# Softmax row sums moved from a ones-matmul on TensorE to GpSimd's sum across partitions

## The chip, the cores and the metric

The kernel runs on one core of one Trainium2 chip. The metric is device time in microseconds (us), where lower is better. Unless a single run is named, a time is the median of several runs. A ratio is the mean time of one kernel's fast runs over that of the other kernel's fast runs of the same rounds, so it is not quite the ratio of the medians that stand beside it. The experiments ran in three sets of rounds, on three chips; the kernel before ran in each set and took 368.65 to 368.81 us (medians), so times of different sets can be compared to a few tenths of a us.

PE is TensorE's matmul stream and PEld its weight loads, DVE is VectorE, ACT is ScalarE, POOL is GpSimd and SP is SyncE.

## The reference

Two independent problems A and B of the same shape are computed and their outputs concatenated. Each is grouped-query attention against a cache, with a projection before and after:

```python
# B=16, Sq=32, D=1024, Hq=32, Hkv=4, Sk=512, Dh=128, all bf16
q = (x @ wq).reshape(B, Sq, Hq, Dh).transpose(0, 2, 1, 3)
k, v = jnp.repeat(k_cache, 8, axis=1), jnp.repeat(v_cache, 8, axis=1)
scores = jnp.einsum("bhqd,bhkd->bhqk", q, k) * Dh ** -0.5
p = softmax(scores, axis=-1)
o = jnp.einsum("bhqk,bhkd->bhqd", p, v)
out = o.transpose(0, 2, 1, 3).reshape(B, Sq, Hq * Dh) @ wo
```

## The kernel before

The attention part is 128 slots. A slot handles one group: one batch row and one key head, with 8 query heads x 32 positions = 256 query columns and 512 keys in 4 chunks of 128. Scores lie transposed, keys on partitions, so the softmax sum runs over chunks (VectorE) and over partitions (a matmul with a constant matrix of ones). Each slot also issues 7 "filler" matmuls of the projections. These are Q-projection matmuls in the first 64 slots (66 in the changed kernel) and output-projection matmuls after them. I call the two stretches the Q stage and the output stage and part them at slot 70.

```python
def partial_sums(i):                      # VectorE: add the 4 key chunks
    p_sb = st[i]["p"]                     # [128, 4 chunks, 256 columns] bf16
    t1 = work.tile([P, 2, QW], FP32, name="t1")
    nc.vector.tensor_tensor(out=t1[:], in0=p_sb[:, 0:2, :], in1=p_sb[:, 2:4, :], op=ALU.add)
    t = work.tile([P, QW], FP32R, name="t")
    nc.vector.tensor_tensor(out=t[:], in0=t1[:, 0, :], in1=t1[:, 1, :], op=ALU.add)
    st[i]["t"] = t

def values(i):
    ...
    for c in range(KC):                   # 4 values matmuls
        nc.tensor.matmul(ob[:, 0:QW], lhsT=v_sb[:, i % GRP, c, :], rhs=d["p"][:, c, :],
                         start=(c == 0), stop=(c == KC - 1))
    nc.tensor.matmul(ob[:, QW:2 * QW], lhsT=ones[:], rhs=d["t"][:], start=True, stop=True)
    ...
    nc.scalar.activation(out=lg[:, q, :], in_=ob[:, QW:2 * QW], func=ACTF.Ln)
    nc.scalar.activation(out=r[:], in_=lg[:, q, :], func=ACTF.Exp, scale=-1.0)
    ...

for i in range(2 * NG):                   # 128 slots
    do_loads(i)
    scores(i)                             # 4 matmuls, then Exp on ScalarE into p_sb
    run(units, 4)                         # 4 filler matmuls
    if i > 0:
        values(i - 1)
    partial_sums(i)
    run(units, 3)                         # 3 filler matmuls
    if i > 0:
        normalize(i - 1)                  # VectorE: oT <- r * ob
```

After the loop a test decides at run time whether a slower general path has to repeat everything. With these inputs it never does.

Of the kernel before, what the change touches and what calls it, by code (L numbers as in the profile page):

```python
# [1 line left out]

# [5 lines left out]

BF16 = mybir.dt.bfloat16
FP32 = mybir.dt.float32  # L10
# [6 lines left out]
P = 128  # L17
# [5 lines left out]
SCALE = float(DH) ** -0.5  # L23

SHIFT = 44.0
ONES = 2.0 ** -75
LIMIT = 20.0


# [143 lines left out]
def kernel(  # L173
# [25 lines left out]
    NG = B * HKV  # L199
    BPT = P // SQ  # L200
    QW = REP * SQ

    out_flat = out.flatten_outer_dims()
    problems = [
# [4 lines left out]
    def fast_path(ok_i):  # L209
        with ExitStack() as fctx:  # L210
            enter = fctx.enter_context
            const = enter(tc.tile_pool(name="const", bufs=1))
            blk = enter(tc.tile_pool(name="blk", bufs=20))
            kv = enter(tc.tile_pool(name="kv", bufs=2))
            work = enter(tc.tile_pool(name="work", bufs=2))
            outp = enter(tc.tile_pool(name="outp", bufs=3))
# [6 lines left out]
            warm = const.tile([P, NW], BF16, name="warm")  # L223
            nc.vector.memset(warm[:], 0.0)  # L224
            ident = const.tile([P, P], BF16, name="ident")
            make_identity(nc, ident[:])
            ones_f = const.tile([P, P], FP32, name="ones_f")
            nc.vector.memset(ones_f[:], ONES)
            ones = const.tile([P, P], FP32R, name="ones")
            nc.vector.tensor_copy(out=ones[:], in_=ones_f[:])  # L230
            one_col = const.tile([P, 1], FP32, name="one_col")
            nc.vector.memset(one_col[:], 1.0)
            shift = const.tile([P, 1], FP32, name="shift")
            nc.vector.memset(shift[:], SHIFT)
            cnt = const.tile([P, 1], FP32, name="cnt")
            nc.vector.memset(cnt[:], 0.0)
            NLR = 2 * NG // GRP
            lall = const.tile([NLR, GRP * QW], FP32, name="lall")


            def blk_tile(shape, name, dtype=BF16):
# [23 lines left out]
            def load_kv(j):  # L265
                pr, jj = divmod(j, NG // GRP)
                k, v = problems[pr][1], problems[pr][2]
                kT = kv.tile([P, GRP, SK], BF16, name="kT")
                v_sb = kv.tile([P, GRP, KC, DH], BF16, name="v_sb")
                if pr == 0:  # L270
                    g, b0 = divmod(jj * GRP, B)
                    ks, vs = k[b0:b0 + GRP, g], v[b0:b0 + GRP, g]
                    for q in range(GRP):
                        nc.sync.dma_start_transpose(out=kT[:, q, :], in_=ks[q])
                else:
                    ks, vs = k[jj], v[jj]
                    nc.sync.dma_start_transpose(
                        out=kT[:], in_=ks.rearrange("g k d -> (g k) d")
                    )
                nc.sync.dma_start(  # L280
                    out=v_sb[:], in_=vs.rearrange("q (p c) d -> p q c d", c=KC)
                )
                kv_tiles[j] = (kT, v_sb)
# [27 lines left out]
            def f_units(pr, tt, nh, last=False):  # L311
                ps = psum.tile([P, NW], FP32, name="f_ps", tag="proj")
                for h in range(HQ):
                    nc.tensor.matmul(  # L314
                        ps[:],
                        lhsT=oT[pr, tt][:, h, :],
                        rhs=wo_tiles[pr, nh, h // REP][:, h % REP, :],
                        start=(h == 0),
                        stop=(h == HQ - 1),
                    )  # L320
                    if h == HQ - 1:
                        o_sb = outp.tile([P, NW], BF16, name="o_sb")
                        nc.vector.tensor_copy(out=o_sb[:], in_=ps[:])  # L323
                        c0 = problems[pr][5] + nh * NW
                        (nc.sync if last else nc.gpsimd).dma_start(  # L325
                            out=out_flat[tt * P:(tt + 1) * P, c0:c0 + NW], in_=o_sb[:]
                        )
                    yield

            def run(units, n):  # L330
# [14 lines left out]
            def scores(i):  # L345
                pr, b, g = where(i)
                kT = kv_tiles[i // GRP][0].rearrange("p q (k c) -> p q c k", c=KC)
                s_ps = psum.tile([P, KC, QW], FP32, name="s_ps", tag="s")
                for c in range(KC):
                    nc.tensor.matmul(  # L350
                        s_ps[:, c, :],
                        lhsT=kT[:, i % GRP, c, :],
                        rhs=qT[pr, g][:, b, :, :].rearrange("p h s -> p (h s)"),
                        start=True,
                        stop=True,
                    )
                p_sb = work.tile([P, KC, QW], BF16, name="p_sb", bufs=3)
                nc.scalar.activation(  # L358
                    out=p_sb[:], in_=s_ps[:], func=ACTF.Exp, bias=shift[:], scale=SCALE
                )  # L360
                st[i] = {"p": p_sb}

            def partial_sums(i):
                p_sb = st[i]["p"]
                t1 = work.tile([P, 2, QW], FP32, name="t1")
                nc.vector.tensor_tensor(
                    out=t1[:], in0=p_sb[:, 0:2, :], in1=p_sb[:, 2:4, :], op=ALU.add
                )
                t = work.tile([P, QW], FP32R, name="t")
                nc.vector.tensor_tensor(  # L370
                    out=t[:], in0=t1[:, 0, :], in1=t1[:, 1, :], op=ALU.add
                )
                st[i]["t"] = t

            ltile = {}

            def values(i):
                d = st[i]
                v_sb = kv_tiles[i // GRP][1]
                ob = psum.tile([P, 2 * QW], FP32, name="ob", tag="ob")  # L380
                for c in range(KC):
                    nc.tensor.matmul(  # L382
                        ob[:, 0:QW],
                        lhsT=v_sb[:, i % GRP, c, :],
                        rhs=d["p"][:, c, :],
                        start=(c == 0),
                        stop=(c == KC - 1),
                    )
                nc.tensor.matmul(  # L389
                    ob[:, QW:2 * QW], lhsT=ones[:], rhs=d["t"][:], start=True, stop=True  # L390
                )
                d["ob"] = ob
                j, q = divmod(i, GRP)
                if q == 0:
                    ltile[j] = work.tile([P, GRP, QW], FP32, name="lg")
                lg = ltile[j]
                nc.scalar.activation(  # L397
                    out=lg[:, q, :], in_=ob[:, QW:2 * QW], func=ACTF.Ln
                )
                r = work.tile([P, QW], FP32, name="r")  # L400
                nc.scalar.activation(out=r[:], in_=lg[:, q, :], func=ACTF.Exp, scale=-1.0)  # L401
                d["r"] = r
                if q == GRP - 1:
                    nc.gpsimd.dma_start(  # L404
                        out=lall[j:j + 1, :],
                        in_=lg[0:1, :, :].rearrange("p q n -> p (q n)"),
                    )

            def normalize(i):
                pr, b, g = where(i)  # L410
# [2 lines left out]
                if (pr, tt) not in oT:  # L413
                    oT[pr, tt] = blk_tile([P, HQ, P], "oT")
                nc.vector.scalar_tensor_tensor(  # L415
                    out=oT[pr, tt][:, g * REP:(g + 1) * REP, bl * SQ:(bl + 1) * SQ],
                    in0=d["r"][:].rearrange("p (h s) -> p h s", s=SQ),
                    scalar=ONES,
                    in1=d["ob"][:, 0:QW].rearrange("p (h s) -> p h s", s=SQ),
                    op0=ALU.mult,  # L420
                    op1=ALU.mult,
                )
# [91 lines left out]
            def at(slot, fn, *args):  # L514
                plan.setdefault(slot, []).append((fn, args))

            for j in range(2, 2 * NG // GRP):
                at(GRP * (j - 1) + 1, load_kv, j)
            for c4 in range(3, 16):
                need = (c4 - 2) * 4 * DC / 7.0  # L520
                at(max(0, int(need) - 10), load_wq, c4 // 8, c4 % 8)
# [3 lines left out]
                nc.sync.dma_start_transpose(out=xT[1][:], in_=B_x.flatten_outer_dims())  # L525

            at(12, load_xT_b)
            for nh in range(NH):
                for hg in range(HKV):
                    at(NG - 12 + nh * 8 + hg * 2, load_wo, 0, nh, hg)  # L530
                    at(NG + 20 + nh * 18 + hg, load_wo, 1, nh, hg)

            def do_loads(i):
                for fn, args in plan.get(i, []):
                    fn(*args)


            for i in range(2 * NG):
                do_loads(i)
                scores(i)  # L540
                run(units, 4)
                if i > 0:
                    values(i - 1)
                partial_sums(i)
                run(units, 3)
                if i > 0:
                    normalize(i - 1)
            run(units, 4)
            values(2 * NG - 1)
            run(units, 4)  # L550
            normalize(2 * NG - 1)


            run(units, 8)
            sq = blk_tile([NLR, GRP * QW], "sq", FP32)
            nc.vector.tensor_tensor(out=sq[:], in0=lall[:], in1=lall[:], op=ALU.mult)
            nc.vector.tensor_scalar(
                out=sq[:], in0=sq[:], scalar1=LIMIT * LIMIT, scalar2=0.0,
# [11 lines left out]
    total = 2 * NG * QW  # L570
    ok = nc.values_load(ok_i[0:1, 0:1], min_val=0, max_val=total,
                        skip_runtime_bounds_check_because="only compared")
    with tc.If(ok < total, preferred_fallthrough_block=False):
        general_path(tc, problems, out_flat)


# [28 lines left out]
```

## Time and profile before

| | before |
|---|---|
| time | 368.72 us, median of 3 runs (368.47 to 369.12) |
| span of the profiled run, granted clock | 366.2 us, 0.995 |
| PE / DVE / ACT / POOL busy | 97 / 67 / 68 / 7% |
| slot length, from scores to scores | 2.52 us, all but the first |
| first scores to last scores; after that to the end | 319.5 us; 24.7 us |

From the page of the kernel before, the busy times (us, share of the span, number of instructions) and the chain of waits that ended last (share of the span by engine, then by engine, tile and line):

```profile
span 366.2 us, 6094 instructions
PE 356.6 (97%) x2236; PEld 225.0 (61%) x2236; DVE 244.2 (67%) x478; ACT 249.2 (68%) x389; POOL 25.1 (7%) x53
...
PE 97%; DVE 0%; ACT 0%; issue 0%
```

The chain is the argument that counts: followed back from the last instruction, it hardly ever leaves PE. A share of busy time alone would not prove that.

The timeline of one slot in the output stage of the kernel before (columns: start in us, duration in us, engine, line, operation, out<-in, shapes, count, and in brackets the idle time before it and what ended it):

```profile
201.66 0.60 PE L382 MATMUL ob<-p_sb,v_sb 128*128 128x256 bf16 x4
...
202.02 0.36 PE L389 MATMUL ob<-t,ones 128*128 128x256 f32 x1
202.15 0.69 DVE L366 TENSOR_TENSOR t_2599<-p_sb 128x512 f32<-128x512 bf16 x1 [0.96 <-ACT p_sb L358]
...
202.22 0.82 PE L314 MATMUL f_ps<-wo_sb,oT 128*128 128x512 bf16 x3
...
202.94 0.43 DVE L370 TENSOR_TENSOR t<-t_2599 128x256 fp32r<-128x256 f32 x1
...
203.29 0.42 DVE L415 SCALAR_TENSOR_TENSOR oT<-r,ob 128x256 bf16<-128x256 f32 x1
...
204.18 0.60 PE L382 MATMUL ob<-p_sb,v_sb 128*128 128x256 bf16 x4
```

The slot repeats after 204.18 - 201.66 = 2.52 us. PE has no bracket: it never idles. The ones-matmul L389 is recorded as 0.36 us, but the next matmul starts 0.20 us after it, so the record overlaps its neighbours. What it costs PE must be read from starts.

### The profile page before, as it was taken

Reading aid. Unit: us, or ns where it says so; the run is one execution under the profiler, and the core shown is the slowest. Engines: PE = TensorE matmul, PEld = TensorE weight load, DVE = VectorE, ACT = ScalarE, POOL = GpSimd, SP = SyncE. Lnnn points to the kernel's source line nnn. Section 1 sums busy time; section 2 is a strip of 40 time slices with the busy share of each in tenths; the row PEclk is TensorE's granted clock in tenths of the full one; section 3 lists DMA queues with packets and bytes.
Section 4 is the critical chain, followed back from the end, with each engine's and each line's share of the span. In section 5 each row is a group of like instructions: output and inputs, shape, how many; then the busy total and the mean of one; then the engine's idle time right before and its main releaser. Section 6 shows DMA issues by size and latency. Waiting matters only on the chain.

```text
span 366.2 us, 6094 instructions
## 1 busy us (share of the span) xinstructions
PE 356.6 (97%) x2236; PEld 225.0 (61%) x2236; DVE 244.2 (67%) x478; ACT 249.2 (68%) x389; POOL 25.1 (7%) x53
## 2 busy tenths in 40 slices
PE   8999999999999999999999999999999999999990
PEld 5556666666666666666666666666666666666540
DVE  2458788887878787888856666666666676666530
ACT  3037777777777777777777777777777777777500
POOL 0000000000000000000001110110001111011100
PEclk9999999999999999999999999999999999999998
DMA  8998796977777784999995555799548974440000
GB/s 274 301 280 242 225 264 147 243 225 219 184 194 183 220 201 115 314 304 310 314 305 138 130 131 142 207 352 198 139 113 287 315 194 117 131 129 17 15 16 21
DMA packets 125974, 71.91 MB, mean 196 GB/s; under 512 B 74641, under 2 KB 124945, under 8 KB 125937
## 3 DMA queue, kind: packets, MB, share of 16 engines
q1 hardware_dynamic: 122848, 68.30, 67.5%
q0 software_dynamic: 1744, 2.10, 2.4%
q10 hardware_dynamic: 1344, 1.05, 0.9%
q8 instruction: 19, 0.31, 0.4%
q14 instruction: 19, 0.15, 0.1%
HBM read 51.38 MB, written 2.10 MB: 146 GB/s over the span
## 4 chain that ended last, share of the span: by engine, by line
PE 97%; DVE 0%; ACT 0%; issue 0%
PE f_ps L314 31%; PE q_ps L297 30%; PE s_ps L350 15%; PE ob L382 15%; PE ob L389 4%; PE warm_ps L446 1%; PE q_ps L469 1%; PE xT_ps L455 0%; ACT xT L460 0%; DVE o_sb L323 0%; DVE xT L459 0%; DVE warm L224 0%; PE ok_ps L563 0%
## 5 line engine op out<-in xcount | busy, mean ns | idle before, releaser
L358 ACT ACTIVATE p_sb<-s_ps,shift 128x1024 bf16<-128x1024 f32 x128 | 142.7, 1115 | 47.5 <-PE s_ps L350 47.5
L314 PE MATMUL f_ps<-wo_sb,oT 128*128 128x512 bf16 x512 | 132.8, 380 | 0.0
L297 PE MATMUL q_ps<-xT,wq_sb 128*128 128x512 bf16 x496 | 128.4, 380 | 0.0
L382 PE MATMUL ob<-p_sb,v_sb 128*128 128x256 bf16 x512 | 76.8, 273 | 0.0
L350 PE MATMUL s_ps<-qT,kT 128*128 128x256 bf16 x512 | 76.8, 273 | 0.0
L397 ACT ACTIVATE lg<-ob 128x256 f32<-128x256 f32 x128 | 49.5, 387 | 39.8 <-PE ob L389 39.8
L350 PEld LDWEIGHTS <-kT 128*128 128x128 bf16 x512 | 57.0, 113 | 28.3 <-issue 0.2
L382 PEld LDWEIGHTS <-v_sb 128*128 128x128 bf16 x512 | 50.1, 98 | 33.1
L314 PEld LDWEIGHTS <-oT 128*128 128x128 bf16 x512 | 44.6, 98 | 32.9
L297 PEld LDWEIGHTS <-wq_sb 128*128 128x128 bf16 x496 | 43.4, 97 | 31.9
L401 ACT ACTIVATE r<-lg 128x256 f32<-128x256 f32 x128 | 53.6, 418 | 4.0
L305 DVE CAST qT<-q_ps 128x512 bf16<-128x512 f32 x62 | 42.7, 689 | 18.2 <-PE q_ps L297 18.0
L415 DVE SCALAR_TENSOR_TENSOR oT<-r,ob 128x256 bf16<-128x256 f32 x128 | 53.5, 418 | 1.6 <-ACT r L401 1.6
L389 PE MATMUL ob<-t,ones 128*128 128x256 f32 x128 | 46.5, 363 | 0.0
L404 POOL DMA_DIRECT2D lall<-lg x32 | 15.9, 496 | 245.4 <-ACT lg L397 245.4
L389 PEld LDWEIGHTS ob<-t,ones 128*128 128x128 f32 x128 | 24.3, 190 | 1.4
L323 DVE CAST o_sb<-f_ps 128x512 bf16<-128x512 f32 x16 | 11.0, 689 | 9.0 <-PE f_ps L314 9.0
L325 POOL DMA_DIRECT2D out_dram<-o_sb x15 | 8.6, 571 | 81.3 <-DVE o_sb L323 81.3
L460 ACT COPY xT<-xT_ps 128x512 bf16<-128x512 bf16 x4 | 2.1, 590 | 5.1 <-DVE xT L459 5.1
L459 DVE COPY xT<-xT_ps 128x512 bf16<-128x512 bf16 x4 | 1.7, 426 | 5.3 <-PE xT_ps L455 5.3
L446 PE MATMUL warm_ps<-warm 128*128 128x512 bf16 x10 | 4.0, 560 | 1.2 <-DVE warm L224 1.2
L469 PE MATMUL q_ps<-xT,wq_sb 128*128 128x256 bf16 x32 | 4.0, 272 | 0.1
(280 smaller groups left out, 158.5 us busy)
## 6 DMA issues: line engine op xcount, KB each, us to landing
v_sb<-in_A_v_cache_dram SPq DMA_DIRECT2D x16, 512.0 KB, 4.2
wq_sb<-in_B_wq_dram SPq DMA_DIRECT2D x8, 1024.0 KB, 6.3
wo_sb<-in_A_wo_dram SPq DMA_DIRECT2D x8, 1024.0 KB, 7.5
v_sb<-in_B_v_cache_dram SPq DMA_DIRECT2D x16, 512.0 KB, 4.2
wo_sb<-in_B_wo_dram SPq DMA_DIRECT2D x8, 1024.0 KB, 8.9
wq_sb<-in_A_wq_dram SPq DMA_DIRECT2D x7, 1024.0 KB, 7.1
out_dram<-o_sb POOLq DMA_DIRECT2D x15, 128.0 KB, 2.4
kT<-in_A_k_cache_dram SPq DMA_TRANSPOSE x64, 3.1
```

The source lines that it names most:

```text
L297: nc.tensor.matmul(ps[:], lhsT=w[:, dc, (h % 4) * DH:(h % 4 + 1) * DH], rhs=xT[pr][:, dc, :], start=(dc == 0), stop=(dc == DC - 1),)
L305: nc.vector.tensor_copy(out=qT[pr, g][:, :, hl, :], in_=ps[:].rearrange("p (b s) -> p b s", s=SQ),)
L314: nc.tensor.matmul(ps[:], lhsT=oT[pr, tt][:, h, :], rhs=wo_tiles[pr, nh, h // REP][:, h % REP, :], start=(h == 0), stop=(h == HQ - 1),)
L323: nc.vector.tensor_copy(out=o_sb[:], in_=ps[:])
L350: nc.tensor.matmul(s_ps[:, c, :], lhsT=kT[:, i % GRP, c, :], rhs=qT[pr, g][:, b, :, :].rearrange("p h s -> p (h s)"), start=True, stop=True,)
L358: nc.scalar.activation(out=p_sb[:], in_=s_ps[:], func=ACTF.Exp, bias=shift[:], scale=SCALE)
L382: nc.tensor.matmul(ob[:, 0:QW], lhsT=v_sb[:, i % GRP, c, :], rhs=d["p"][:, c, :], start=(c == 0), stop=(c == KC - 1),)
L389: nc.tensor.matmul(ob[:, QW:2 * QW], lhsT=ones[:], rhs=d["t"][:], start=True, stop=True)
L397: nc.scalar.activation(out=lg[:, q, :], in_=ob[:, QW:2 * QW], func=ACTF.Ln)
L401: nc.scalar.activation(out=r[:], in_=lg[:, q, :], func=ACTF.Exp, scale=-1.0)
L404: nc.gpsimd.dma_start(out=lall[j:j + 1, :], in_=lg[0:1, :, :].rearrange("p q n -> p (q n)"),)
L415: nc.vector.scalar_tensor_tensor(out=oT[pr, tt][:, g * REP:(g + 1) * REP, bl * SQ:(bl + 1) * SQ], in0=d["r"][:].rearrange("p (h s) -> p h ...
```

## The change

The intent is to take the 128 ones-matmuls off TensorE, which bounds the kernel. GpSimd, only 7% busy until now, sums across partitions for two groups at a time. VectorE's two adds, which read two SBUF inputs each, become one reduce with a single input. Because the sums now come later, the values of a group are computed four slots behind its scores. Smaller parts: the identity matrix is made on VectorE, weight loads are rescheduled, the last output tile is copied and stored in halves, and the general path is laid out as the fall-through block of its branch.

```diff
+    LAG = 4
...
-                p_sb = work.tile([P, KC, QW], BF16, name="p_sb", bufs=3)
+                p_sb = work.tile([P, KC, QW], BF16, name="p_sb", bufs=LAG + 2)
...
             def partial_sums(i):
-                t1 = ...; tensor_tensor(out=t1, in0=p_sb[:, 0:2, :], in1=p_sb[:, 2:4, :])
-                t = ...;  tensor_tensor(out=t, in0=t1[:, 0, :], in1=t1[:, 1, :])
+                j, q = divmod(i, 2)
+                if q == 0:
+                    tsum[j] = work.tile([P, 2, QW], FP32, name="t")
+                nc.vector.tensor_reduce(
+                    out=tsum[j][:, q, :],
+                    in_=p_sb[:].rearrange("p c n -> p n c"),
+                    axis=AX.X, op=ALU.add,
+                )
+                if q == 1:
+                    sums[j] = work.tile([P, 2, QW], FP32, name="sums", bufs=3)
+                    nc.gpsimd.partition_all_reduce(sums[j], tsum.pop(j), channels=P,
+                                                   reduce_op=bass_isa.ReduceOp.add)
+            def reciprocals(j):                      # Ln, then Exp, on 512 columns
...
             def values(i):
-                nc.tensor.matmul(ob[:, QW:2 * QW], lhsT=ones[:], rhs=d["t"][:], ...)
...
+            for i in range(total_slots + LAG):
+                live = i < total_slots
+                if live:
+                    do_loads(i); scores(i)
+                if i % 2 == 1 and i >= 3:
+                    if i >= 5:
+                        keep_logs(i // 2 - 2)
+                    if i // 2 - 1 < NG:
+                        reciprocals(i // 2 - 1)
+                run(units, 4 if live else 5)
+                if i >= LAG:
+                    values(i - LAG)
+                if live:
+                    partial_sums(i)
+                run(units, 3 - (i % 4 == 3) if live else 3)
+                if i >= LAG:
+                    normalize(i - LAG)
...
-    with tc.If(ok < total, preferred_fallthrough_block=False):
+    with tc.If(ok < total, preferred_fallthrough_block=True):
```

More of the change, by code (lines that the diff above doesn't have):

```diff
@@ L4 @@
 import concourse.tile as tile
-from concourse import bass_utils, mybir
+from concourse import bass_isa, bass_utils, mybir
 from concourse._compat import with_exitstack
@@ L25 @@
 SHIFT = 44.0
-ONES = 2.0 ** -75
+DOWN = 2.0 ** -75
 LIMIT = 20.0
@@ L212, in fast_path @@
             const = enter(tc.tile_pool(name="const", bufs=1))
-            blk = enter(tc.tile_pool(name="blk", bufs=20))
+            blk = enter(tc.tile_pool(name="blk", bufs=19))
             kv = enter(tc.tile_pool(name="kv", bufs=2))
@@ L225, in fast_path @@
             ident = const.tile([P, P], BF16, name="ident")
-            make_identity(nc, ident[:])
-            ones_f = const.tile([P, P], FP32, name="ones_f")
-            nc.vector.memset(ones_f[:], ONES)
-            ones = const.tile([P, P], FP32R, name="ones")
-            nc.vector.tensor_copy(out=ones[:], in_=ones_f[:])
+            col = const.tile([P, P], BF16, name="col")
+            row = const.tile([P, P], BF16, name="row")
+            nc.vector.memset(row[:], 1.0)
+            nc.vector.tensor_tensor_scan(
+                out=col[:], data0=row[:], data1=row[:], initial=0.0, op0=ALU.mult, op1=ALU.add
+            )
+            nc.vector.transpose(out=row[:], in_=col[:])
+            nc.vector.memset(ident[:], 0.0)
+            for k in range(0, P, 32):
+                d = slice(k, k + 32)
+                nc.vector.tensor_tensor(
+                    out=ident[d, d], in0=row[d, d], in1=col[d, d], op=ALU.is_equal
+                )
             one_col = const.tile([P, 1], FP32, name="one_col")
@@ L236, in fast_path @@
             nc.vector.memset(cnt[:], 0.0)
-            NLR = 2 * NG // GRP
-            lall = const.tile([NLR, GRP * QW], FP32, name="lall")
+            NLR = NG
+            lall = const.tile([NLR, 2 * QW], FP32, name="lall")
             def blk_tile(shape, name, dtype=BF16):
@@ L268, in load_kv @@
                 kT = kv.tile([P, GRP, SK], BF16, name="kT")
-                v_sb = kv.tile([P, GRP, KC, DH], BF16, name="v_sb")
+                v_sb = kv.tile([P, GRP, KC, DH], BF16, name="v_sb", bufs=3)
                 if pr == 0:
@@ L322, in f_units @@
                         o_sb = outp.tile([P, NW], BF16, name="o_sb")
-                        nc.vector.tensor_copy(out=o_sb[:], in_=ps[:])
-                        c0 = problems[pr][5] + nh * NW
-                        (nc.sync if last else nc.gpsimd).dma_start(
-                            out=out_flat[tt * P:(tt + 1) * P, c0:c0 + NW], in_=o_sb[:]
-                        )
+                        rows, c0 = slice(tt * P, (tt + 1) * P), problems[pr][5] + nh * NW
+                        if last:
+                            hw = NW // 2
+                            nc.vector.tensor_copy(out=o_sb[:, :hw], in_=ps[:, :hw])
+                            nc.scalar.copy(out=o_sb[:, hw:], in_=ps[:, hw:])
+                            nc.sync.dma_start(
+                                out=out_flat[rows, c0:c0 + hw], in_=o_sb[:, :hw]
+                            )
+                            nc.scalar.dma_start(
+                                out=out_flat[rows, c0 + hw:c0 + NW], in_=o_sb[:, hw:]
+                            )
+                        else:
+                            nc.vector.tensor_copy(out=o_sb[:], in_=ps[:])
+                            nc.gpsimd.dma_start(
+                                out=out_flat[rows, c0:c0 + NW], in_=o_sb[:]
+                            )
                     yield
@@ L361, in scores @@
                 st[i] = {"p": p_sb}
+            tsum, sums, logs, rcp = {}, {}, {}, {}
             def partial_sums(i):
                 p_sb = st[i]["p"]
-                t1 = work.tile([P, 2, QW], FP32, name="t1")
-                nc.vector.tensor_tensor(
-                    out=t1[:], in0=p_sb[:, 0:2, :], in1=p_sb[:, 2:4, :], op=ALU.add
-                )
-                t = work.tile([P, QW], FP32R, name="t")
-                nc.vector.tensor_tensor(
-                    out=t[:], in0=t1[:, 0, :], in1=t1[:, 1, :], op=ALU.add
-                )
@@ L373, in partial_sums @@
-                st[i]["t"] = t
-            ltile = {}
+                j, q = divmod(i, 2)
[4 more added lines that the diff above has]
+                    in_=p_sb[:].rearrange("p c n -> p n c"),
+                    axis=AX.X,
+                    op=ALU.add,
+                )
+                if q == 1:
+                    sums[j] = work.tile([P, 2, QW], FP32, name="sums", bufs=3)
+                    nc.gpsimd.partition_all_reduce(
+                        sums[j][:].rearrange("p q n -> p (q n)"),
+                        tsum.pop(j)[:].rearrange("p q n -> p (q n)"),
+                        channels=P,
+                        reduce_op=bass_isa.ReduceOp.add,
+                    )
@@ new lines, in reciprocals, with keep_logs @@
+            def reciprocals(j):
+                lg = sums.pop(j)
+                nc.scalar.activation(out=lg[:], in_=lg[:], func=ACTF.Ln, scale=DOWN)
+                rcp[j] = work.tile([P, 2, QW], FP32, name="r")
+                nc.scalar.activation(out=rcp[j][:], in_=lg[:], func=ACTF.Exp, scale=-1.0)
+                logs[j] = lg
+            def keep_logs(j):
+                nc.scalar.dma_start(
+                    out=lall[j:j + 1, :],
+                    in_=logs.pop(j)[0:1, :, :].rearrange("p q n -> p (q n)"),
+                )
@@ L377, in values @@
             def values(i):
-                d = st[i]
                 v_sb = kv_tiles[i // GRP][1]
-                ob = psum.tile([P, 2 * QW], FP32, name="ob", tag="ob")
+                ob = psum.tile([P, QW], FP32, name="ob", tag="ob")
                 for c in range(KC):
                     nc.tensor.matmul(
-                        ob[:, 0:QW],
+                        ob[:],
                         lhsT=v_sb[:, i % GRP, c, :],
-                        rhs=d["p"][:, c, :],
+                        rhs=st[i]["p"][:, c, :],
@@ L388, in values @@
                     )
-                nc.tensor.matmul(
-                    ob[:, QW:2 * QW], lhsT=ones[:], rhs=d["t"][:], start=True, stop=True
-                )
-                d["ob"] = ob
-                j, q = divmod(i, GRP)
-                if q == 0:
-                    ltile[j] = work.tile([P, GRP, QW], FP32, name="lg")
-                lg = ltile[j]
-                nc.scalar.activation(
-                    out=lg[:, q, :], in_=ob[:, QW:2 * QW], func=ACTF.Ln
-                )
-                r = work.tile([P, QW], FP32, name="r")
-                nc.scalar.activation(out=r[:], in_=lg[:, q, :], func=ACTF.Exp, scale=-1.0)
-                d["r"] = r
-                if q == GRP - 1:
-                    nc.gpsimd.dma_start(
-                        out=lall[j:j + 1, :],
-                        in_=lg[0:1, :, :].rearrange("p q n -> p (q n)"),
-                    )
+                st[i]["ob"] = ob
             def normalize(i):
@@ L416, in normalize @@
                     out=oT[pr, tt][:, g * REP:(g + 1) * REP, bl * SQ:(bl + 1) * SQ],
-                    in0=d["r"][:].rearrange("p (h s) -> p h s", s=SQ),
-                    scalar=ONES,
-                    in1=d["ob"][:, 0:QW].rearrange("p (h s) -> p h s", s=SQ),
+                    in0=rcp[i // 2][:, i % 2, :].rearrange("p (h s) -> p h s", s=SQ),
+                    scalar=DOWN,
+                    in1=d["ob"][:].rearrange("p (h s) -> p h s", s=SQ),
                     op0=ALU.mult,
@@ L517, in fast_path @@
             for j in range(2, 2 * NG // GRP):
-                at(GRP * (j - 1) + 1, load_kv, j)
+                at(GRP * (j - 1), load_kv, j)
             for c4 in range(3, 16):
@@ L527, in fast_path @@
             at(12, load_xT_b)
-            for nh in range(NH):
-                for hg in range(HKV):
-                    at(NG - 12 + nh * 8 + hg * 2, load_wo, 0, nh, hg)
-                    at(NG + 20 + nh * 18 + hg, load_wo, 1, nh, hg)
+            for hg in range(HKV):
+                at(52 + 2 * hg, load_wo, 0, 0, hg)
+                at(68 + 4 * hg, load_wo, 0, 1, hg)
+                at(85 + 4 * hg, load_wo, 1, 0, hg)
+                at(104 + 2 * hg, load_wo, 1, 1, hg)
             def do_loads(i):
@@ L535, in do_loads @@
                     fn(*args)
-            for i in range(2 * NG):
-                do_loads(i)
-                scores(i)
-                run(units, 4)
-                if i > 0:
-                    values(i - 1)
-                partial_sums(i)
-                run(units, 3)
-                if i > 0:
-                    normalize(i - 1)
-            run(units, 4)
-            values(2 * NG - 1)
-            run(units, 4)
-            normalize(2 * NG - 1)
+            total_slots = 2 * NG
+            for i in range(total_slots + LAG):
+                live = i < total_slots
+                if live:
+                    do_loads(i)
+                    scores(i)
+                if i % 2 == 1 and i >= 3:
[11 more added lines that the diff above has]
+                    normalize(i - LAG)
             run(units, 8)
-            sq = blk_tile([NLR, GRP * QW], "sq", FP32)
+            sq = blk_tile([NLR, 2 * QW], "sq", FP32)
             nc.vector.tensor_tensor(out=sq[:], in0=lall[:], in1=lall[:], op=ALU.mult)
```

## The prediction

> **What bounds the kernel now.** TensorE. The chain of waits is PE for 97% of the span, the windows view shows PE busy 100% from 20 to 345 us, and the timeline repeats a slot per query group (4 scores, 4 filler projections, 4 values, 1 ones-matmul, 3 filler) of 2.52 us. All slots but the first are 2.52 us, so nothing else ever holds PE up. Per slot the others need (lines view): VectorE 0.69 + 0.43 + 0.42 and 7/8 of a 0.69 cast, about 2.1 us; ScalarE 1.115 + 0.387 + 0.418 = 1.92; GpSimd almost nothing.
>
> **Removed.** 128 fp32r ones-matmuls (L389). Their busy sum is 46.5 us, but that is not their price: the 363 ns records overlap their neighbours. From starts in the timeline: one values matmul follows another after 109 ns; the ones-matmul starts 29 ns after the last of them and the next filler 207 ns later. Four values and ones hold PE 3 x 109 + 29 + 207 = 563 ns, four values alone 436. Gain 127 ns per slot, 128 x 0.127 = 16.3 us, all on the critical path. The slot becomes about 2.39 us; the filler is unchanged in total.
>
> **Added, against 2.39 us.**
> - VectorE: two adds (0.69 + 0.43) become one reduce over 1024 elements. The adds give 1.07 ns per output column plus 0.15 us; the Trainium skill (VectorE: DVE Perf Modes, the perf-mode tier table) gives tensor_reduce only the 1x mode, so I estimate 1.24 us. VectorE then needs 1.24 + 0.42 + 0.60 = 2.26 us per slot, 94%, in the first half (Q projections), less later. Tight but fitting, unless the reduce's 512-byte stride slows it.
> - GpSimd: one all-reduce of 128x512 fp32 per two slots; it must stay under 4.79 us. Neither trace nor page gives its duration. The Trainium skill (GPSIMD Engine Reference, Performance versus the Vector engine, and Performance pitfalls) puts one pass at 1.03 to 2.9 cycles per element, 0.44 to 1.24 us for 512 columns; for three or four passes I estimate 1.5 to 5, likely 3 us. Above about 3.4 us ScalarE waits for the sums, which the lag of four slots hides; above 4.79 us GpSimd is the bound.
> - ScalarE: Ln and Exp in pairs of 512 columns, about 0.66 us each (0.418 at 256, plus 0.95 ns per further column from the 0.387 and 1.115): 0.66 instead of 0.80 us per slot, plus small DMA issues.
> - DMA: same bytes, 5% less time; its share is well below full outside 150 to 200 us.
>
> **Ends.** Identity on VectorE is ready before x lands (4.2 us). The last output in halves saves about 0.3 us. The branch: SyncE idles 1.6 us after its first branch and 2.5 us after its second; the new layout may move this by 1 us either way; I count -0.3.
>
> **Sum.** 368.7 - 16.3 - 0.6 + 0.7 for small VectorE stalls = 352.5 us. Range 347 to 360. Faster by over 2%: 0.84; within 2%: 0.08; slower by over 2%: 0.08.
>
> **What shows it right.** No ones-matmul; slots of about 2.39 us, PE over 95% of the chain; the reduce near 1.24 us; 64 all-reduces under 4.8 us; VectorE above 90% busy from 20 to 180 us, without PE gaps.
>
> **What would make it wrong.** A reduce above 1.35 us makes VectorE the bound until about 190 us (each further 0.1 us costs about 7 us); an all-reduce over 4.8 us makes GpSimd the bound (64 us per extra us); wo or K loads arriving late after the reordering.

## The result, and the profile after

The changed kernel took 385.41 us (median of 4 runs, 385.31 to 386.03) against 368.92 us for the kernel before: ratio 1.0452, 95% interval 1.0433 to 1.047. It is slower by 4.5%, and the predicted 352.5 us was wrong in direction.

| | before | after |
|---|---|---|
| span of the profiled run, granted clock | 366.2 us, 0.995 | 383.7 us, 0.995 |
| mean slot, Q stage (slots 4 to 70) | 2.520 us | 2.674 us |
| mean slot, output stage (slots 70 to 127) | 2.520 us | 2.534 us |
| first scores to last scores; after that to the end | 319.5; 24.7 us | 329.5; 32.3 us |

The same parts of the page of the changed kernel:

```profile
span 383.7 us, 5506 instructions
PE 347.8 (91%) x2068; PEld 210.3 (55%) x2108; DVE 335.1 (87%) x356; ACT 215.1 (56%) x262; POOL 214.7 (56%) x83
...
DVE 58%; PE 13%; ACT 11%; issue 10%; POOL 6%; ACTq 0%; DVEq 0%; POOLq 0%
DVE t L390 42%; DVE qT L314 8%; DVE oT L437 7%; POOL sums L398 6%; ACT p_sb L378 5%; PE q_ps L306 5%; PE f_ps L323 4%; ACT sums L407 3%; ACT r L409 3%; DVE o_sb L344 1%; PE warm_ps L468 1%; PE q_ps L491 1%; PE ob L422 1%; PE s_ps L370 1%; PE xT_ps L477 0%
```

PE has left the chain, and 42% of the span is one line of VectorE, the new reduce L390. The costliest groups of the changed kernel (line, engine, operation, shapes and count | busy us, mean ns of one | idle us before them and what ended it):

```profile
L398 POOL PARTITION_ALL_REDUCE sums<-t x64 | 206.7, 3230 | 142.4 <-DVE t L390 108.8
L390 DVE TENSOR_REDUCE t<-p_sb 128x256 f32<-128x1024 bf16 x128 | 247.9, 1937 | 13.3 <-ACT p_sb L378 13.2
L378 ACT ACTIVATE p_sb<-s_ps,shift 128x1024 bf16<-128x1024 f32 x128 | 136.4, 1103 | 20.0 <-PE s_ps L370 19.7
...
L422 PE MATMUL ob<-p_sb,v_sb 128*128 128x256 bf16 x512 | 76.7, 272 | 10.8 <-DVE oT L437 9.4
```

GpSimd's sum takes 3.23 us for two slots, close to the guess of 3, and it is within the budget of 4.79. But the reduce takes 1.94 us where 1.24 was predicted. The timeline of the changed kernel in the Q stage shows what that does:

```profile
60.36 1.93 DVE L390 TENSOR_REDUCE t<-p_sb 128x256 f32<-128x1024 bf16 x1
...
62.21 0.68 DVE L314 CAST qT<-q_ps 128x512 bf16<-128x512 f32 x1
62.80 0.41 DVE L437 SCALAR_TENSOR_TENSOR oT<-r,ob 128x256 bf16<-128x256 f32 x1
62.94 0.38 PE L306 MATMUL q_ps<-xT,wq_sb 128*128 128x512 bf16 x1 [1.00 <-DVE qT L314]
```

VectorE works without a gap, and PE idles 1.00 us until the cast has freed the projection's PSUM buffer. The next instruction on VectorE starts 1.85 us after the start of a reduce, 0.60 after that of a cast and 0.33 after that of a normalize (medians). A Q-stage slot has 6.75/8 of a cast on average, so VectorE needs 1.85 + 0.33 + 0.84 x 0.60 = 2.69 us, and the measured slot is 2.674. In this stage VectorE's throughput is the whole story.

In the output stage there is only 6.75/32 of an output cast per slot, so VectorE needs 1.85 + 0.33 + 0.13 = 2.31 us, no more than PE's 2.33. Yet the slots are 2.534. The waits there are of another kind. The fence holds lines of the view of waits of the changed kernel (who waited for whom: us in total, times, longest us), for PE, DVE and ACT in turn, first three lines for the Q stage and then three for the output stage:

```profile
PE q_ps L306 <- DVE qT L314: 12.3, 18, 1.4
...
DVE t L390 <- ACT p_sb L378: 0.8, 2, 0.5
...
ACT sums L407 <- POOL sums L398: 60.0, 32, 2.4
...
PE ob L422 <- DVE oT L437: 6.3, 16, 0.7
...
DVE t L390 <- ACT p_sb L378: 12.4, 17, 1.1
...
ACT sums L407 <- POOL sums L398: 51.8, 29, 2.9
```

In the output stage ScalarE waits for GpSimd, the reduce waits for ScalarE, and PE waits for the normalize: a circle rather than one busy engine. ScalarE's wait alone does not mark it, for it is as long in the Q stage (60.0 us). What is new in the output stage is that VectorE then waits for ScalarE (12.4 us against 0.8). Experiment 10 below tests it.

The sum in round figures, per the two tables: PE was relieved of 127 slots x 0.127 = 16 us. Stalls cost 66 x (2.674 - 2.331) = 22.6 us in the Q stage and 57 x (2.534 - 2.331) = 11.6 us in the output stage, where 2.331 is the slot without a stall that run 4 below shows (6.75 fillers and 8 other matmuls, 6.75 x 0.216 + 8 x 0.109 = 2.330). That is 34 us lost against 16 won, and it accounts for the 17.5 us by which the span grew, to within a rough 1 us. The quarter filler less per slot (32 x 0.216 = 6.9 us) only moved from the loop to the end. Two effects at the end are not in the sum and nearly cancel: from the last matmul's end to the end of the span there are 6.86 us instead of 8.26 (experiment 11), and the long reduce costs 1.6 us after the last scores (32.3 us, against 30.6 in run 4).

### The profile page after: what moved, and what is told of

It reads as the page before. It is cut to its first block, busy times and chain, and to the rows that moved or that the text cites. A ratio compares the mean times of both kernels' runs of the same rounds, so it can differ in the third digit from the quotient of the medians.

```text
span 383.7 us, 5506 instructions
## 1 busy us (share of the span) xinstructions
PE 347.8 (91%) x2068; PEld 210.3 (55%) x2108; DVE 335.1 (87%) x356; ACT 215.1 (56%) x262; POOL 214.7 (56%) x83
## 4 chain that ended last, share of the span: by engine, by line
DVE 58%; PE 13%; ACT 11%; issue 10%; POOL 6%; ACTq 0%; DVEq 0%; POOLq 0%
DVE t L390 42%; DVE qT L314 8%; DVE oT L437 7%; POOL sums L398 6%; ACT p_sb L378 5%; PE q_ps L306 5%; PE f_ps L323 4%; ACT sums L407 3%; ACT r L409 3%; DVE o_sb L344 1%; PE warm_ps L468 1%; PE q_ps L491 1%; PE ob L422 1%; PE s_ps L370 1%; PE xT_ps L477 0%
## 5 line engine op out<-in xcount | busy, mean ns | idle before, releaser
L398 POOL PARTITION_ALL_REDUCE sums<-t x64 | 206.7, 3230 | 142.4 <-DVE t L390 108.8
L390 DVE TENSOR_REDUCE t<-p_sb 128x256 f32<-128x1024 bf16 x128 | 247.9, 1937 | 13.3 <-ACT p_sb L378 13.2
L378 ACT ACTIVATE p_sb<-s_ps,shift 128x1024 bf16<-128x1024 f32 x128 | 136.4, 1103 | 20.0 <-PE s_ps L370 19.7
L323 PE MATMUL f_ps<-wo_sb,oT 128*128 128x512 bf16 x492 | 127.6, 379 | 1.0
L407 ACT ACTIVATE sums<-sums 128x512 f32<-128x512 f32 x64 | 40.3, 630 | 119.9 <-POOL sums L398 117.7
L306 PEld LDWEIGHTS <-wq_sb 128*128 128x128 bf16 x496 | 48.4, 98 | 40.1 <-issue 11.0
L323 PEld LDWEIGHTS <-oT 128*128 128x128 bf16 x512 | 50.0, 98 | 32.1
L409 ACT ACTIVATE r<-sums 128x512 f32<-128x512 f32 x64 | 40.4, 631 | 2.0
```

Source lines behind the costliest of these rows:

```text
L306: nc.tensor.matmul(ps[:], lhsT=w[:, dc, (h % 4) * DH:(h % 4 + 1) * DH], rhs=xT[pr][:, dc, :], start=(dc == 0), stop=(dc == DC - 1),)
L323: nc.tensor.matmul(ps[:], lhsT=oT[pr, tt][:, h, :], rhs=wo_tiles[pr, nh, h // REP][:, h % REP, :], start=(h == 0), stop=(h == HQ - 1),)
L378: nc.scalar.activation(out=p_sb[:], in_=s_ps[:], func=ACTF.Exp, bias=shift[:], scale=SCALE)
L390: nc.vector.tensor_reduce(out=tsum[j][:, q, :], in_=p_sb[:].rearrange("p c n -> p n c"), axis=AX.X, op=ALU.add,)
L398: nc.gpsimd.partition_all_reduce(sums[j][:].rearrange("p q n -> p (q n)"), tsum.pop(j)[:].rearrange("p q n -> p (q n)"), channels=P, reduc ...
L407: nc.scalar.activation(out=lg[:], in_=lg[:], func=ACTF.Ln, scale=DOWN)
```

## The experiments

My theory R is that the loss is the reduce: VectorE is held for 1.85 us where the two adds held it 0.73 + 0.34 = 1.07 (medians, from the starts of the instructions in the kernel before). The rivals are G, that GpSimd's work slows VectorE or holds things up, and, within R, three causes: the power-of-two step (B), any large step (S), or the reduce as an operation (O). All edits are against the changed kernel unless "kernel before" is said.

### 1. The reduce alone, without GpSimd (kernel before)

```diff
-                tensor_tensor ...; tensor_tensor ...      # the two adds
+                nc.vector.tensor_reduce(out=t[:], in_=p_sb[:].rearrange("p c n -> p n c"),
+                                        axis=AX.X, op=ALU.add)
```

> The kernel before with only the two adds replaced by the one strided reduce; the ones-matmul stays and GpSimd stays idle. Theory R (the reduce at 1.94 us, 1.85 us of VectorE's time, is the loss): VectorE needs 1.85 + 0.33 + 7/8 x 0.60 = 2.70 us per slot in the Q stage against PE's 2.52, so the Q slots rise to about 2.70 and the time by about 66 x 0.18 = 12 us, to 380 to 382 us; the output stage stays at 2.52. Rival G (GpSimd's sum slows VectorE or holds things up): the reduce is short without it and the time stays within 1% of 368.7.

Measured: 380.57 us against 368.65, ratio 1.0323 (1.0302 to 1.0343). Correct. The group of the reduce in this run:

```profile
L367 DVE TENSOR_REDUCE t<-p_sb 128x256 fp32r<-128x1024 bf16 x128 | 247.0, 1931 | 9.1 <-ACT p_sb L358 9.1
```

The reduce is just as long with GpSimd idle. Q slots are 2.683 us, output slots 2.520. R holds and G falls as the explanation of the long reduce. In the changed kernel itself, reduces that overlap an all-reduce entirely (61 of them) have a median of 1931 ns and those that overlap none (33) 1943 ns.

### 2. The two adds back, with GpSimd's sum

```diff
-                nc.vector.tensor_reduce(out=tsum[j][:, q, :], in_=p_sb[:].rearrange("p c n -> p n c"), ...)
+                t1 = work.tile([P, 2, QW], FP32, name="t1", bufs=1)
+                nc.vector.tensor_tensor(out=t1[:], in0=p_sb[:, 0:2, :], in1=p_sb[:, 2:4, :], op=ALU.add)
+                nc.vector.tensor_tensor(out=tsum[j][:, q, :], in0=t1[:, 0, :], in1=t1[:, 1, :], op=ALU.add)
```

> The changed kernel with the two two-input adds back in place of the reduce (the scratch tile single-buffered for space); everything else as changed. Theory R: slots fall to about 2.33, about 350 us, if the adds keep their 0.69 and 0.43 us beside GpSimd. Rival P (two SBUF inputs share a port with GpSimd's reads): the adds that overlap an all-reduce are stretched, up to its 3.2 us, and the slot is 2.7 us or more; the time is then 385 us or more.

Measured: 389.84 us against 368.65, ratio 1.0575 (1.0557 to 1.0593). Correct. The rival P won, with slots of 2.73 us in the Q stage and 2.56 in the output stage. The timeline of this run around one all-reduce:

```profile
222.64 3.23 POOL L399 PARTITION_ALL_REDUCE sums<-t  x1 [1.73 <-DVE t L394]
...
223.27 2.16 DVE L391 TENSOR_TENSOR t<-p_sb 128x512 f32<-128x512 bf16 x1 [0.55 <-ACT p_sb L378]
...
225.53 0.43 DVE L394 TENSOR_TENSOR t<-t 128x256 f32<-128x256 f32 x1
```

The first add, 0.69 us alone, took 1.77 to 2.76 us in the 63 cases in which it fell wholly under an all-reduce. In all 63 it ended 2.77 to 2.79 us after the all-reduce had started, whenever it had begun itself. So the add behaves here as if it had to wait until about 2.79 - 0.69 = 2.1 us into the 3.23 us of the all-reduce. The Trainium skill (SBUF - State Buffer, "Who interferes with whom") says that a VectorE instruction with two SBUF inputs contends with a GpSimd instruction that reads SBUF, and that tensor_reduce never does. Both agree with these runs: 63 adds were stretched, and the reduces took 1931 ns under an all-reduce against 1943 without (run 1). The same page ("SBUF: two separate sides") says that the port pair over which the two contend is held for the whole instruction; the 2.1 of 3.23 us differ from that. So the change's choice of a single-input reduce had a good reason: going back to the adds is no remedy.

### 3. Another distance between the chunks

```diff
-                p_sb = work.tile([P, KC, QW], BF16, ...)
+                p_all = work.tile([P, KC, QW + 8], BF16, ...)
+                p_sb = p_all[:, :, 0:QW]
```

> The changed kernel with the key chunks 264 columns apart instead of 256 (528 bytes instead of 512). Theory B (a power-of-two step meets the same memory bank each time): the reduce falls to about 1.24 us and the time to about 352 us. Theory S (any step far over an element costs the same) and theory O (the reduce itself costs 1.75 ns per element): the reduce stays at 1.94 us and the time at 385 us.

Measured: 385.5 us, ratio 1.0456 (1.0438 to 1.0473), the reduce 1933 ns. Correct. Theory B falls.

### 4. The same reduce over neighbours (wrong result)

```diff
-                    in_=p_sb[:].rearrange("p c n -> p n c"),
+                    in_=p_sb[:].rearrange("p c (m e) -> p (c m) e", e=KC),
```

> The changed kernel whose reduce takes four neighbouring columns instead of four chunks: same element count, step 1. The result is wrong on purpose. Theory S or B (the step is the cost): the reduce falls to about 1.24 us and the time to 350 to 356 us. Theory O (reduce itself): 1.94 us and 385 us as changed.

Measured: 350.63 us against 368.65, ratio 0.9507 (0.9491 to 0.9523). It adds up the wrong elements. The comparison with the reference passed all the same (also in runs 7 and 8), presumably because the sums of neighbouring columns are close on these inputs. The group of the reduce in this run:

```profile
L390 DVE TENSOR_REDUCE t<-p_sb 128x256 f32<-128x1024 bf16 x128 | 155.8, 1217 | 56.4 <-ACT p_sb L378 54.4
```

Same operation, same element count, same GpSimd work, and the reduce is 1.217 us. Q slots are 2.361 us and output slots 2.331, so both stages are PE's again. Once this one number is right, the time lies in the predicted range (347 to 360 us) and PE holds 94% of the chain, where over 95% was forecast. VectorE is busy 85% of the time from 20 to 180 us, where the prediction had above 90%: it counted 1.24 us for the reduce and 0.42 for a normalize, which hold VectorE 1.14 and 0.33 from start to start where nothing waits. Against the changed kernel the short reduce is worth 385.4 - 350.6 = 34.8 us, as the sum of the stalls above said. Theory O falls: what was long was the way the reduce reads.

### 5. Keys innermost: a correct kernel with step 1 for the reduce

```diff
-                p_sb = work.tile([P, KC, QW], BF16, name="p_sb", bufs=LAG + 2)
+                p_nc = work.tile([P, QW, KC], BF16, name="p_sb", bufs=LAG + 2)
+                p_sb = p_nc[:].rearrange("p n c -> p c n")
...
-                    in_=p_sb[:].rearrange("p c n -> p n c"),
+                    in_=st[i]["nc"][:],
```

> The changed kernel with the exponentials stored column by column, the four key chunks next to each other (ScalarE writes with an 8-byte step, the values matmul reads its moving operand with an 8-byte step, the reduce reads step 1). Correct result. Theory S (the step of the reduce is all that went wrong) with free steps on the other two engines: reduce 1.22 us, slots 2.33 to 2.36 us, about 350.5 us, faster than both kernels. Rival M (the step moves the cost): the values matmuls start more than 109 ns apart, or the exponential takes more than 1.11 us; each further 10 ns per values matmul would cost 512 x 0.010 = 5 us.

Measured: 426.23 us, ratio 1.1565 (1.1544 to 1.1586). Correct, and rival M won clearly. The groups of this run:

```profile
L379 ACT ACTIVATE p_sb<-s_ps,shift 128x1024 bf16<-128x1024 f32 x128 | 310.5, 2554 | 13.8 <-PE s_ps L370 13.8
L391 DVE TENSOR_REDUCE t<-p_sb 128x256 f32<-128x1024 bf16 x128 | 156.1, 1220 | 135.2 <-ACT p_sb L379 132.3
L423 PE MATMUL ob<-p_sb,v_sb 128*128 128x256 bf16 x512 | 136.6, 401 | 3.5 <-DVE oT L438 2.4 <-DMA kT<-in_B_k_cache_dram 0.9
```

The reduce is short, but the 8-byte step went to the two others. ScalarE's exponential, writing with it, went from 1.10 to 2.55 us, and the values matmuls, reading with it, started 227 ns apart (median) instead of 109.

### 6. The same layout, with the step on ScalarE's read

```diff
-                    out=p_sb, in_=s_ps[:], func=ACTF.Exp, ...
+                    out=p_nc[:], in_=s_ps[:].rearrange("p c n -> p n c"), func=ACTF.Exp, ...
```

> As the one before, but ScalarE reads the scores from PSUM with a step of 1024 bytes and writes step 1. If a strided read is dearer for ScalarE than a strided write, the exponential is longer here than there; over about 1.7 us per group ScalarE would be the bound. If not, the same time as the one before within 1%.

Measured once: 409.98 us, correct. The exponential is back at 1114 ns: reading the scores from PSUM with a step of 1024 bytes cost ScalarE nothing here, writing to SBUF with a step of 8 bytes cost it 1.45 us. What stays is PE: values matmuls 226 ns apart, slots 2.80 us, and 2.331 + 4 x (0.226 - 0.109) = 2.80. The expectation was missed: it allowed a longer exponential or the time of run 5 within 1%, and the time is 3.8% less than that of run 5.

### 7 and 8. How far apart may the four elements be? (wrong results on purpose)

```diff
-                    out=tsum[j][:, q, :],
-                    in_=p_sb[:].rearrange("p c n -> p n c"),
+                    out=tsum[j][:, q, :].rearrange("p (m s) -> p m s", s=S),       # S = 2, then 8
+                    in_=p_sb[:].rearrange("p c n -> p (c n)").rearrange("p (m e s) -> p m s e", e=KC, s=S),
```

> The changed kernel, the reduce's four elements 4 bytes apart (wrong result on purpose). Theory L (the cost comes with each new 16-byte line that is touched, as the Trainium skill, SBUF - State Buffer, says of strides): four elements within 16 bytes, the reduce stays near 1.22 us. Theory N (any step other than 1): about 1.94 us.

> The same with 16 bytes between the four elements (wrong result on purpose). Theory L: every element in another 16-byte line, so the full 1.94 us as with 512 bytes. If the cost needs a larger distance than 16 bytes, the reduce is shorter than 1.94 us.

Measured once each: 351.04 us with 4 bytes between the elements, 386.91 us with 16. The group of the reduce with 4 bytes:

```profile
L390 DVE TENSOR_REDUCE t<-p_sb 128x256 f32<-128x1024 bf16 x128 | 155.8, 1217 | 55.9 <-ACT p_sb L378 54.2
```

and with 16 bytes:

```profile
L390 DVE TENSOR_REDUCE t<-p_sb 128x256 f32<-128x1024 bf16 x128 | 248.9, 1945 | 13.1 <-ACT p_sb L378 13.0
```

Sixteen bytes cost as much as 512, four bytes nothing. Theory N falls, and theory L fits: with run 9 below, where a step of 8 bytes cost nothing, the limit lies between 8 and 16 bytes. No run separates a line of 16 bytes from a step of 16 bytes. The Trainium skill (SBUF - State Buffer, Specifications) gives SBUF lines of 16 bytes and asks for at least two hits per line for full bandwidth; for VectorE's reads these runs agree. For PE's moving operand they do not: in runs 5 and 6 it had two hits per line and took twice as long.

### 9. Blocks of four columns: a layout for all three engines

```diff
-                p_sb = work.tile([P, KC, QW], BF16, name="p_sb", bufs=LAG + 2)
+                p_sb = work.tile([P, QW // 4, KC, 4], BF16, name="p_sb", bufs=LAG + 2)
...
-                    out=p_sb[:], in_=s_ps[:], func=ACTF.Exp, ...
+                    out=p_sb[:], in_=s_ps[:].rearrange("p c (b r) -> p b c r", r=4), func=ACTF.Exp, ...
...
-                    out=tsum[j][:, q, :],
-                    in_=p_sb[:].rearrange("p c n -> p n c"),
+                    out=tsum[j][:, q, :].rearrange("p (b r) -> p b r", r=4),
+                    in_=p_sb[:].rearrange("p b c r -> p b r c"),
...
-                        ob[:], ... rhs=st[i]["p"][:, c, :],
+                        ob[:].rearrange("p (b r) -> p b r", r=4), ... rhs=st[i]["p"][:, :, c, :],
```

> The changed kernel with the exponentials stored in blocks of four columns by four key chunks: the reduce's step is 8 bytes (two of its four elements per 16-byte line), the values matmul reads runs of 8 bytes every 32 bytes, ScalarE reads the scores with a step and writes step 1, which was free in the run before. Correct result. From the runs so far: VectorE paid nothing at 4 elements per line and 0.72 us at one per line; PE paid double at 2 neighbours per line (227 against 109 ns). If VectorE needs two hits per line and PE four, the reduce is 1.22 us, the values matmuls stay 109 ns apart and the time is about 350.5 us, 5% faster than the kernel before. If PE also pays for the broken runs (above 150 ns apart), the slots are 2.5 us or more and the time 372 us or more; if VectorE pays, the reduce is between 1.3 and 1.9 us and Q slots follow it.

Measured: 354.07 us (353.01 to 354.45) against 368.76, ratio 0.9598 (0.958 to 0.9615). Correct, and faster than both kernels. From the page and the groups of this run:

```profile
PE 343.1 (97%) x2108; PEld 210.3 (60%) x2108; DVE 251.5 (71%) x356; ACT 218.6 (62%) x262; POOL 214.5 (61%) x83
...
PE 91%; DMA 3%; ACT 2%; DVE 1%; ACTq 0%; issue 0%; SPq 0%; DVEq 0%
...
L390 DVE TENSOR_REDUCE t<-p_sb 128x256 f32<-128x1024 bf16 x128 | 155.9, 1218 | 57.7 <-ACT p_sb L378 56.5
L378 ACT ACTIVATE p_sb<-s_ps,shift 128x1024 bf16<-128x1024 f32 x128 | 141.6, 1109 | 82.4 <-PE s_ps L370 82.4
L422 PE MATMUL ob<-p_sb,v_sb 128*128 128x256 bf16 x512 | 79.9, 277 | 0.2 <-DVE oT L437 0.2
```

PE is back at 91% of the chain. The reduce reads two of its elements per 16-byte line and pays nothing; the exponential pays nothing. The values matmuls start 116 ns apart instead of 109, which is 512 x 0.007 = 3.6 us, about the distance to the 350.63 us of run 4 (3.4 us). That lies between the two cases of the expectation. Whether PE needs four hits per line, or whether its cost goes with the length of an unbroken run, these runs do not separate.

### 10. A longer lag

```diff
-    LAG = 4
+    LAG = 5                                   # and output buffers 3 -> 2 for space
...
-                if i % 2 == 1 and i >= 3:        # reciprocals of pair j in slot 2j + 3
+                if i % 2 == 0 and i >= 4:        # reciprocals of pair j in slot 2j + 4
```

> The changed kernel with the reciprocals one slot later and values five slots behind instead of four (one more buffer of exponentials; output buffers two instead of three). In the output stage VectorE needs only 1.85 + 0.33 + 0.13 = 2.31 us per slot, yet the slots are 2.534. Theory C (a circle of waits: sum on GpSimd, Ln and Exp, two exponentials, two reduces, next sum, about 10.1 us for four slots): a longer lag opens it, output slots fall to 2.34 to 2.38, Q slots stay at 2.67, time about 375 to 377 us. Rival D (VectorE's throughput alone holds the output stage): slots and time stay within 1% of 385.4.

Measured: 371.91 us against 368.76, ratio 1.0086 (1.007 to 1.0101). Correct. Output slots fell from 2.534 to 2.331 us, Q slots stayed near (2.656 against 2.674), the reduce was 1940 ns. The time is below the 375 to 377 us that theory C gave. Theory C holds and D falls. The windows view (stretch in us and its length; busy us of PE, PEld, DVE, ACT and POOL; granted clock, DMA share, GB/s) of the changed kernel for the two stages:

```profile
31.00:206.00 175.00, 157.87 (x947) 97.10 (x964) 174.22 (x183) 109.11 (x132) 105.16 (x34) 1.00 0.74 194
207.00:351.00 144.00, 135.46 (x823) 84.43 (x839) 132.08 (x127) 91.95 (x113) 97.27 (x41) 1.00 0.70 193
```

and of this run:

```profile
31.00:206.00 175.00, 159.59 (x970) 97.64 (x969) 175.00 (x184) 112.56 (x133) 106.38 (x34) 1.00 0.73 193
207.00:339.00 132.00, 132.00 (x837) 84.42 (x835) 131.57 (x127) 96.07 (x114) 96.93 (x42) 1.00 0.77 212
```

In the output stage of the changed kernel neither PE (135 of 144) nor VectorE (132 of 144) is full; with the longer lag both are (132 of 132). That is what a circle of waits looks like in a table of busy times, and what its removal looks like. In the Q stage VectorE is full in both. The view of waits of this run for the output stage, for DVE and ACT in turn, confirms it:

```profile
DVE t L390 <- ACT p_sb L378: 0.4, 2, 0.2
...
ACT p_sb L378 <- PE s_ps L370: 33.8, 29, 1.3
```

ScalarE's wait for the sums (51.8 us) is gone, the reduce's wait for ScalarE fell from 12.4 to 0.4 us, and PE has no wait in this stage any more. Besides the buffers, two things were moved at once, the values by one slot and the reciprocals by one slot in ScalarE's order; which of them opens the circle was not tested. The lag is a separate loss of about 57 x (2.534 - 2.331) = 11.6 us, but the long reduce feeds it: in run 4, with the old lag and a short reduce, output slots are 2.331 as well.

### 11. The branch layout alone (kernel before)

```diff
-    with tc.If(ok < total, preferred_fallthrough_block=False):
+    with tc.If(ok < total, preferred_fallthrough_block=True):
```

> The kernel before with the general path as fall-through block, nothing else. I expect a change at the end alone, after the last projection: within 1 us of 368.7 either way, so a ratio between 0.997 and 1.003.

Measured: 366.51 us (5 runs) against 368.76, ratio 0.9945 (0.9932 to 0.9959). Correct. It is a small gain, and larger than I had allowed. The slots are 2.52 us as before. From the last matmul's end to the end of the span there are 8.26 us in the kernel before and 6.58 here. In the kernel before, SyncE stands still twice after a branch (1.6 and 2.7 us from the branch to its next instruction); here it does once (2.6 us).

## Why the prediction was wrong

- **What bounds before: right.** PE, 2.52 us per slot.
- **What the ones-matmul is worth: right.** 127 ns per slot from starts, not the 363 ns of its record. Run 4 agrees: it is 18.0 us faster than the kernel before, of which the branch layout can explain 2.2 (run 11), and its slots of 2.331 us would be 2.385 with the quarter filler that was moved, where 2.39 was predicted.
- **GpSimd: right.** 3.23 us per pair against "likely 3 us", below 4.79. Its sums do not lengthen the reduce. The "three or four passes" behind the 3 us were a guess that no run tests, so that it came so close is luck; that it stayed under the bound is what counted.
- **ScalarE: right in size.** Ln and Exp take 0.63 us each, predicted 0.66. But "Above about 3.4 us ScalarE waits for the sums, which the lag of four slots hides" failed, as a consequence of the reduce: at 3.23 us ScalarE already waited for the sums (51.8 us in the output stage), since two long reduces stand in front of each sum, and four slots did not hide it (run 10). With the short reduce of run 4 the same wait is 16.5 us over the whole span instead of 117.7, and PE loses nothing by it.
- **The step that failed: "so I estimate 1.24 us" for the reduce, with "Tight but fitting, unless the reduce's 512-byte stride slows it".** It measured 1.94 us. I took the slope of 1.07 ns per column from the two adds, which read with step 1, and gave the stride little weight. So VectorE needed 2.69 us per slot in the Q stage, not 2.26, and became the bound there. Run 4 (step 1) gives 1.217 us. Runs 3, 7, 8 and 9 show that neither the power of two nor a larger distance matters: a step of 8 bytes, with two elements per 16-byte line, was free, and a step of 16 bytes, with one, cost as much as the reduce's 512.
- **The size of the consequence: right in form, too coarse.** "each further 0.1 us costs about 7 us" above 1.35 us would give 5.9 x 7 = 41 us on top of the base. The runs showed 22.6 us in the Q stage and 11.6 from the circle in the output stage, which the prediction did not have. The chances given to a slower kernel, 0.08, were far too small for a risk that was named.
- **Ends: undersized.** The branch layout was worth 2.2 us by itself on the kernel before, where I counted 0.3. No run isolates the identity matrix or the halved last output.

## What to carry to other kernels

When an instruction's time is estimated from another's, compare how the two read, not only how many elements they touch; a named stride is a cost to be settled before the estimate, not a clause after it. A layout shared by several engines has a price on each of them, so look for a blocking that gives each reader enough neighbours per 16-byte line, and put the permutation where it was free here (ScalarE reading PSUM). When no engine is full in a stage and PE still waits, look for a circle of waits, and lengthen the lag before looking for throughput.

## What the Trainium skill lacked or had wrong

- VectorE: DVE Perf Modes, perf-mode tier table: it gives tensor_reduce one mode and no word on its inner step. The skill as a whole is not silent on steps (its SBUF lines, next point), so what is missing in this place is the pointer. Here 128x1024 bf16 to 128x256 took 1.22 us with steps of 2, 4 or 8 bytes and 1.94 us with 16, 512 or 528.
- SBUF - State Buffer, Specifications: two hits per 16-byte line were enough for VectorE (1.22 us in run 9), not for PE's moving operand (8-byte step: 227 ns between matmul starts against 109; runs of four columns, 8 bytes in every 32: 116 ns) and not for ScalarE's write (8-byte step: 2.55 us against 1.10).
- SBUF - State Buffer, "SBUF: two separate sides": an add with two SBUF inputs waited until about 2.1 us into GpSimd's 3.23 us all-reduce, not until its end as the page has it (63 cases, all ending 2.77 to 2.79 us after its start).
- GPSIMD Engine Reference: it has no duration for the all-reduce across partitions (its one time for a sum over partitions, in Cross-partition, is for tensor_reduce, another instruction); here 128x512 fp32 took 3.23 us, in 64 cases within 12 ns.
- I found no page that names a ScalarE write to SBUF with an 8-byte step as slow (2.55 us against 1.10 for 128x1024) or says that its PSUM read with a 1024-byte step is not (1.11 us).
